# Attention of batches 2 to 7 one slot earlier in an attention + MoE kernel, with its second score half and first global scores two slots earlier

## The chip, the cores and the metric

The kernel runs on 1 core of one Trainium2 chip. The metric is device time in microseconds (us), the median of the runs shown. PE is TensorE's matmul stream, DVE VectorE, ACT ScalarE, POOL GpSimd, SP the engine whose queue issues the DMAs.

## The reference

Attention over 8 batches and 8 heads, with 512 local and 32 global positions and head dimension 64, and behind it a MoE-like layer with one expert:

```python
s_g = scale * q_g @ k_all^T;   out_g = softmax(s_g) @ v_all       # global rows see all 544 keys
s_l = concat(q_l @ k_g^T, q_l @ k_l^T where |i - j| <= 32)         # local rows: global keys and a band
out_l = softmax(s_l) @ concat(v_g, v_l)
x = concat(out_g, out_l) as (8 * 544, 512)
h = x @ w_in            # 512 -> 2048
out = (h * cos(h)) @ w_out   # 2048 -> 512
```

All is float32. The kernel keeps the accuracy by splitting operands into a high and a low float16 part, and multiplies three products (high x high, high x low, low x high) for each.

## The kernel before, in words

**MoE.** The local rows are handled in 16 chunks of 256 rows (chunk c belongs to batch c // 2), and a 17th chunk holds the global rows of all batches. A chunk has 8 blocks j, each of 256 of the 2048 hidden columns. For a block, `m1_a` (L812) makes ph with 24 matmuls of 256 columns; `m1_b` (L834, L835) and `m1_c` (the table function `Sin`, through the helper at L434) make u and w; `m1_d` squares w on POOL, multiplies into gf on DVE (L852), casts gf to gh on ACT (L856) and makes gl on POOL; `m2_a` (L872) adds 12 matmuls of 512 columns into the chunk's two output tiles po. `m2_b` evacuates po to o on DVE (L881) and ACT (L883) at the chunk's end. ph has three PSUM buffers, po two.

**Attention.** The 8 heads of a batch are four pairs p. For a pair, `sc_a` (L536) makes the scores ps, in two halves (i = 0 and i = 2), each for two heads, in fp32 on tiles of 64 rows; `sc_b` (L554) reads them on DVE with mask and running minimum; `sc_c` takes the exponentials on ACT, `sc_d` (L601, L602) the high and low planes on ACT and DVE, `sc_e` transposes them by DMA; `av_a` (L654) multiplies with the values into acc, and `av_b` (L674, L675) writes xh and xl, the input of the MoE. For two pairs g, `g_a` (L693) makes global scores gps in two parts (k = 0 of 288 and k = 1 of 256 columns), and `g_f` (L748) the global product gacc. ps, acc, gps, gacc and the small matmul pm_v (L468, `spread_b`) share the tag att, three PSUM buffers. For each batch `load_v` loads the values (one buffer vr), `v_a` takes their maximum on DVE (L490), `v_b` spreads it over the partitions by pm_v, and `v_d` makes vh on ACT and vl on DVE (L521).

**What sets the order.** Time is cut into slots. Slot 8 c + j is that of block j of chunk c, and its po matmuls stand three slots later. `at(slot, phase, f, ...)` puts each step of the attention into a slot and a phase in it. For batches 2 to 7 `steady(t)` gives a pair's slots by offsets from t, with t = 16 (b - 1) + T0 + 4 p: first score half at t - 7 (`s_sc0`), second at t - 5 (`s_sc2`), first global part at t - 6 (`s_gs0`), second at t - 4, exponentials t - 4, planes t - 3, transposes t - 1, product at t. Batch b's first MoE chunk has slot 16 b, so with T0 = 3 the last pair's product stands in the slot just before it. Batches 0 and 1 have a table of their own (`tight`). From these ranks a scheduler lays out each engine's instruction order at build time; on the chip each engine runs its own order and waits for semaphores.

```python
        for b in range(2, B):
            t = 16 * (b - 1) + T0
            for p in range(NPAIR):
                attn_pair(b, p, steady(t + 4 * p))
```

Of the kernel before, what the change touches and what calls it, by code (L numbers as in the profile page):

```python
# [8 lines left out]
F16 = mybir.dt.float16  # L9
# [5 lines left out]
AF = mybir.ActivationFunctionType  # L15
ALU = mybir.AluOpType
# [3 lines left out]
P = 128  # L20
# [4 lines left out]
D = 64  # L25
# [17 lines left out]
EXPMASK = 0x7F800000  # L43
MAGIC = 1.5 * 2.0**23
KAPPA = 3
T0 = 3
SPLIT = 256
PL = 1
MF = 1
TS = 1  # L50
# [7 lines left out]
NS = NJ // 2  # L58
# [10 lines left out]
WLV = 0  # L69
SW = 256  # L70
LO = "m01v2345"
J7 = "xl3"
L7 = -5
PS = 128
MR = 2
SR = (1,)
AR = (1,)
WH = "AAAAAAAADDDDDDDD"
# [3 lines left out]
NAL = -1.0 / math.sqrt(D)  # L82
s_load = -10
s_sc0 = -7
s_sc2 = -5
s_ex = -4
s_sd = -3
s_tr = -1
s_vd = -8
s_av = 0  # L90
s_gs0 = -6
s_gs1 = -4
s_gd = -3
s_ge = -1
# [13 lines left out]
U1 = 2  # L108
SP1 = 2
VD1 = 1  # L110
PO = 1
WOPH = 9
# [14 lines left out]

def body(tc, qf, v, wi, wo, mask, out):
    nc = tc.nc
    lag = 3  # L130

    from contextlib import ExitStack

    with ExitStack() as ctx:
# [98 lines left out]
        def decode(y, raw, s, low_after=None, join_after=None):  # L233

            hi, lo = raw.bitcast(F32)[..., 1::2], raw[..., 0::2]
            nc.scalar.activation(y, hi, AF.Prelu, scale=s, alpha=2.0**32)
            low = nc.vector.tensor_scalar(
                lo, lo, 29, 1, op0=ALU.logical_shift_right, op1=ALU.bitwise_or
            )
            behind(low.ins, low_after)  # L240
            join = nc.vector.scalar_tensor_tensor(  # L241
                y.bitcast(U32), y.bitcast(U32), 3, lo,
                op0=ALU.logical_shift_left, op1=ALU.bitwise_or,
            )
# [85 lines left out]
        def w_in_piece(k):  # L330
            kc = k // 2
            parts = wfs.pop(("raw", k))
            n = 1024 // len(parts)
            for a, raw in enumerate(parts):
                c = slice(k % 2 * 1024 + a * n, k % 2 * 1024 + a * n + n)
                z = raw.bitcast(F32)[:, 1::2]
                decode(z, raw, wfs["s", kc], join_after=J7 if k == 7 else "xs" if k == 6 else "dx" if k >= 4 else None)
                split_w(wi_h[:, kc, c], wi_l[:, kc, c], z)

        wfi = cp.tile([P, 2], F32, name="wfi")  # L340

# [64 lines left out]
        def w_out_piece(j):  # L406
            if j < 8:
                raw = wo_raw[:, j]
            else:
                raw = w2.tile([P, 1024], U32, tag="raw", name=f"raw_wo{j}")  # L410
                nc.sync.dma_start(raw.bitcast(I64), wo[j * P : (j + 1) * P])
            z = w2.tile([P, DM], F32, tag="wy", name=f"z_wo{j}")
            decode(z, raw, wsc, low_after="wsc")
            split_w(wo_h[:, j], wo_l[:, j], z, j % 4 < WLV, WH[j], SW)

        def w_out_done():
            m = ap_.tile([P, 1], F32, tag="wm", name="wm_o")
# [158 lines left out]
        def sc_d(b, p, i):  # L576
# [190 lines left out]
        mp = None  # L767
# [49 lines left out]
        def gf_tile(c, j, n):  # L817
            if GFW and c >= 2 and j % GFW == GFW - 1:
                return w2.tile([P, n], F32, tag="wy", name=f"gf_{c}_{j}")
            return mp.tile([P, n], F32, tag="gf", name=f"gf_{c}_{j}", bufs=GFB)  # L820
# [24 lines left out]
        def m1_d(c, j):  # L845
            w = st.pop(("u", c, j))[1]
            n = w.shape[-1]
            gh = mp.tile([P, n], F16, tag="gh", name=f"gh_{c}_{j}", bufs=4)
            gl = mp.tile([P, n], F16, tag="gl", name=f"gl_{c}_{j}", bufs=4)
            pool_tt(w, w, w, ALU.mult, PS if c < 2 else n)  # L850
            gf = gf_tile(c, j, n)
            nc.vector.scalar_tensor_tensor(  # L852
                gf, w, 0.5, st.pop(("ph", c, j)).rearrange("p a b -> p (a b)"),
                op0=ALU.subtract, op1=ALU.mult,
            )
            nc.scalar.copy(gh, gf)  # L856
            pool_tt(gl, gf, gh, ALU.subtract, PS if c < 2 else n)
            st["g2", c, j] = (gh, gl)

        def m2_a(c, j):  # L860
# [43 lines left out]
        def at(slot, phase, f, *a, pr=None):  # L904
            e = (phase, len(ev[slot]), f, a)
            ev[slot].append(e)
            pr = (slot, phase) if pr is None else pr if isinstance(pr, tuple) else (pr, phase)
            rank[slot, e[1]] = pr + (slot, e[1])
# [3 lines left out]
        def attn_pair(b, p, o):  # L912
            if b:
                at(o["load"], PJ, load_qk, b, p)
            attn_rest(b, p, o)

        def attn_rest(b, p, o):
            for i in range(4):
                at(o["sc"][i], PA, sc_a, b, p, i)
                at(o["sc"][i], PA if o["tight"] else PC, sc_b, b, p, i)  # L920
                at(o["ex"], PI, sc_c, b, p, i)
                at(o["sd"], PF, sc_d, b, p, i)
                at(o["tr"][i], PA2, sc_e, b, p, i)
            at(o["vd"], PF2, v_d, b, p)
            at(o["av"], PA, av_a, b, p)
            at(o["av"] if b else -6, PF, av_b, b, p)
            if p % 2:
                g = p // 2
                for k in range(2):
                    at(o["gs"][k], PA, g_a, b, g, k)  # L930
                    at(o["gs"][k], PA if o["tight"] else PC, g_b, b, g, k)
                at(o["ex"], PI, g_c, b, g)
                at(o["gd"], PF2, g_d, b, g)
                at(o["ge"], PA2, g_e, b, g)
                at(o["gf"] if b else GF0, PG, g_f, b, g)
                at(o["gf"] if b else GF0, PH2, g_g, b, g)
# [36 lines left out]
        for k in range(8):  # L973
            if 2 <= k < 4:
                at(WL[1], PJ, w_in_load, k)
            at(WE + k - WM, PH2, w_in_max, k, pr=W0 + k - WM)
            at(WE + k if k < 4 else -13 if k < 6 else -11 if k < 7 else L7, PK, w_in_piece, k, pr=(W0 + k, PJ))
            if k < 4:
                at(WE + k, PJ, w_in_load, k + 4, pr=W0 + k if k < 3 else W0 - 1)
# [5 lines left out]
            at(WOE + k // WOS if k < 12 else -10, PJ, w_out_max, k, pr=(WO + k // WOS, PI))  # L985
        at(-9, PB, w_out_done, pr=(WO + 7, PI))
        for k in range(16):
            at(k // 2 + PO, WOPH, w_out_piece, k)
        at(LV1, PJ, load_v, 1)
        at(VA1, PF, v_a, 1)  # L990
        at(VA1, PG, v_b, 1)
        at(VA1, PG2, v_c, 1)
        for p in range(NPAIR):
            attn_pair(1, p, tight(U1 + SP1 * p, VD1 + p))
        for b in range(2, B):
            t = 16 * (b - 1) + T0
            at(t + s_v, PA0, load_v, b)
# [8 lines left out]
            (-7, -4, -9, -8, -6, -2, -10),  # L1006
        )[MF]
        for c in range(NC + 1):
            at(NS * c, -11, chunk_scales, c)
            for j in range(NS):  # L1010
                s = NS * c + j
                if c == 0 and j < JS:
                    for kc in range(NPAIR):
                        at(-5 + kc, PJ, m1_a, c, j, kc)
                else:
                    at(s, ma, m1_a, c, j)
                at(s, mb, m1_b, c, j)
# [88 lines left out]
```

## Time and profile before

| | us |
|---|---|
| runs (median 951.33) | 951.33, 949.33, 951.34 |
| profiled execution, its time | 949.26 |
| span of that execution | 947.5 |
| PE busy in the span | 896.2 (95%) |
| ACT busy | 660.6 (70%) |
| DVE busy | 578.5 (61%) |
| POOL busy | 421.9 (45%) |

The span runs from the program's first instruction to the end of its last; the time of the execution holds 1.8 us beside it. Matmuls are pipelined, and a matmul's end is modelled, so that a busy PE need not be PE at its peak: in a chain of waits the start of each group, and the distance to the next one's start, tell what a group takes.

### The profile page before, as it was taken

How to read it: one execution, taken by the hardware profiler on the slowest of the kernel's cores; microseconds unless marked ns; L12 is line 12 of the kernel's file. 1: busy time of each engine (PE TensorE's matmuls, PEld its weight loads, DVE VectorE, ACT ScalarE, POOL GpSimd, SP SyncE). 2: the span in 40 equal slices, each digit the busy share in tenths (PEclk: the TensorE clock that was granted, in tenths of full speed). 3: DMA queues.
4: the chain of work that ended last, by engine and by line, in shares of the span. 5: the costliest groups of instructions: out<-in, count | busy, mean ns of one | idle time of the engine just before them, and what ended most of it. 6: DMA issues, size and time to landing. Idle time of an engine off the chain costs nothing.

```text
span 947.5 us, 19962 instructions
## 1 busy us (share of the span) xinstructions
PE 896.2 (95%) x7643; PEld 597.5 (63%) x7643; DVE 578.5 (61%) x1568; ACT 660.6 (70%) x1419; POOL 421.9 (45%) x508
## 2 busy tenths in 40 slices
PE   6757888999999999999999999999999999999995
PEld 4446564666666666666666666666666666666663
DVE  5999989757565647566656656565746555423231
ACT  6887798877787777767777677777777766434341
POOL 5867977453333243434343334324343434444441
PEclk8558999999999999999999999999999999999998
DMA  9936256645242524444352635251533333000000
GB/s 366 389 133 192 82 149 153 130 122 134 43 118 48 154 53 96 85 123 112 65 116 56 179 46 134 46 160 38 117 57 92 62 68 59 24 1 24 1 23 23
DMA packets 155176, 96.41 MB, mean 102 GB/s; under 512 B 141000, under 2 KB 141128, under 8 KB 153288
## 3 DMA queue, kind: packets, MB, share of 16 engines
q1 hardware_dynamic: 155080, 95.13, 40.2%
q8 instruction: 60, 0.98, 0.4%
q14 instruction: 36, 0.29, 0.1%
HBM read 51.59 MB, written 8.91 MB: 64 GB/s over the span
## 4 chain that ended last, share of the span: by engine, by line
PE 82%; DVE 7%; ACT 3%; POOL 3%; DMA 2%; issue 1%; SPq 0%; ACTq 0%; POOLq 0%
PE ph L812 36%; PE po L872 35%; PE ps L536 5%; PE acc L654 4%; PE gps L693 2%; DVE planes L602 1%; PE gacc L748 1%; DMA raw_wo<-wo 1%; DMA vr<-v 1%; ACT t L434 1%; POOL wo_hl L222 1%; POOL vl L518 1%; DVE z_wo L241 1%; POOL wi_l L222 1%; DVE raw_wi L241 1%
## 5 line engine op out<-in xcount | busy, mean ns | idle before, releaser
L872 PE MATMUL po<-wo_hl,gh 128*128 128x512 f16 x1088 | 321.8, 380 | 9.7 <-POOL wo_hl L222 9.7
L812 PE MATMUL ph<-xh,wi_h 128*128 128x256 f16 x1024 | 280.4, 274 | 3.3 <-DVE gf L852 3.3
L812 PE MATMUL ph<-xl,wi_h 128*128 128x256 f16 x1024 | 279.8, 273 | 0.5 <-DVE xl L675 0.5
L812 PE MATMUL ph<-xh,wi_l 128*128 128x256 f16 x1024 | 279.8, 273 | 0.0
L222 POOL TENSOR_TENSOR gl<-gf,gh 128x512 f16<-128x512 f32 (+1 forms) x184 | 173.8, 955 | 230.2 <-ACT gh L856 229.3
L222 POOL TENSOR_TENSOR w<-w 128x512 f32<-128x512 f32 (+1 forms) x184 | 152.9, 841 | 248.3 <-ACT w L434 236.0
L812 PEld LDWEIGHTS <-wi_h 128*128 128x128 f16 x2176 | 206.0, 98 | 56.2 <-issue 19.6
L872 PE MATMUL po<-wo_hl,gl 128*128 128x512 f16 x544 | 201.5, 381 | 0.0
L872 PEld LDWEIGHTS <-gh 128*128 128x128 f16 x1088 | 106.8, 98 | 103.0 <-issue 2.3
L856 ACT CAST gh<-gf 128x512 f16<-128x512 f32 x136 | 83.3, 613 | 123.8 <-DVE gf L852 122.8
L852 DVE SCALAR_TENSOR_TENSOR gf<-w,ph 128x512 f32<-128x512 f32 x136 | 93.0, 684 | 113.7 <-POOL w L222 113.0
L434 ACT ACTIVATE w<-u,ca 128x512 f32<-128x512 f32 x136 | 97.9, 721 | 87.5 <-DVE u L835 84.8
L835 DVE SCALAR_TENSOR_TENSOR u<-u,cm,ph 128x512 f32<-128x512 f32 x136 | 101.2, 744 | 94.5 <-ACT u L834 94.5
L434 ACT ACTIVATE t<-t,mn 128x192 f32<-128x192 f32 (+1 forms) x256 | 116.6, 456 | 6.4 <-DVE mn L554 6.0
L812 PEld LDWEIGHTS <-wi_l 128*128 128x128 f16 x1088 | 106.7, 98 | 14.2 <-issue 1.4
L602 DVE SCALAR_TENSOR_TENSOR planes<-t,sm,planes 128x192 f16<-128x192 f32 (+1 forms) x232 | 100.4, 493 | 13.9 <-ACT planes L601 13.2
L834 ACT ACTIVATE u<-ph,cm 128x512 f32<-128x512 f32 x136 | 92.0, 677 | 18.8 <-PE ph L812 18.8
L872 PEld LDWEIGHTS <-gl 128*128 128x128 f16 x544 | 53.3, 98 | 73.0 <-issue 10.7
L554 DVE CUSTOM_DVE_ANT_0 t<-ps,msk 128x192 f32<-128x192 f32 (+1 forms) x256 | 82.8, 366 | 11.4 <-PE ps L536 10.4
L601 ACT ACTIVATE planes<-t,sm 128x192 f16<-128x192 f32 (+1 forms) x232 | 86.1, 455 | 2.2 <-DVE gsm L720 2.2
L536 PE MATMUL ps<-qkr 64*128 64x192 f32 (+1 forms) x496 | 73.0, 382 | 6.1 <-DMA qkr<-qf 5.4
L434 ACT ACT_TABLE_LOAD x58 | 74.4, 1283 | 3.7 <-DVE u L835 2.0
(149 smaller groups left out, 919.9 us busy)
## 6 DMA issues: line engine op xcount, KB each, us to landing
qkr<-qf SPq DMA_DIRECT2D x31, 608.0 KB, 5.0
vr<-v SPq DMA_DIRECT2D x8, 1280.0 KB, 6.6
out<-o SPq DMA_DIRECT2D x34, 256.0 KB, 2.1
raw_wi<-wi SPq DMA_DIRECT2D x6, 1024.0 KB, 13.2
wo_hl<-wo SPq DMA_DIRECT2D x8, 512.0 KB, 11.5
raw_wm<-wo SPq DMA_DIRECT2D x8, 512.0 KB, 4.2
raw_wo<-wo SPq DMA_DIRECT2D x8, 512.0 KB, 4.0
raw_wi<-wi SPq DMA_DIRECT2D x4, 512.0 KB, 12.3
```

The lines of the kernel that those rows point to most:

```text
L222: nc.gpsimd.tensor_tensor(o[..., c], a[..., c], b[..., c], op=op)
L434: ins = nc.scalar.activation(*a, **k).ins
L536: nc.tensor.matmul(pt[h][:, c], q[r, QZ[j] : QZ[j] + P], k[r, z : z + w], start=True, stop=True, skip_group_check=True,)
L554: nc.vector.tensor_tensor_reduce(t[:, h], pt[h], msk[:, MOFF[i] : MOFF[i] + w], NAL, 3.0e38, ALU.add, ALU.min, mn[:, h : h + 1],)
L601: a = nc.scalar.activation(hi, t[:, h], AF.Identity, scale=r)
L602: d = nc.vector.scalar_tensor_tensor(lo, t[:, h], r, hi, op0=ALU.mult, op1=ALU.subtract)
L812: nc.tensor.matmul(ph[:, a], w[:, kc, f], x[:, kc, q], start=first and ip == 0, stop=last and ip == 2, skip_group_check=True,)
L834: nc.scalar.activation(u, ph, AF.Identity, bias=m)
L835: nc.vector.scalar_tensor_tensor(u, u, m, ph, op0=ALU.subtract, op1=ALU.subtract)
L852: nc.vector.scalar_tensor_tensor(gf, w, 0.5, st.pop(("ph", c, j)).rearrange("p a b -> p (a b)"), op0=ALU.subtract, op1=ALU.mult,)
L856: nc.scalar.copy(gh, gf)
L872: nc.tensor.matmul(po[k], g[:, a * CT + k * P : a * CT + (k + 1) * P], w[:, 2 * j + a], start=(j == 0 and i == 0), stop=(j == NS - 1 and i ...
```

## The change

Three constants: T0 from 3 to 2 moves all of the attention of batches 2 to 7 (loads of values and queries too) one slot ahead of the MoE; `s_sc2` from -5 to -6 and `s_gs0` from -6 to -7 move the second score half and the first global scores one slot more, so that a pair's two score halves stand in slots next to each other and the first global scores in the slot of the first half. The other constants (LG, LGC, GB, PSQ, PSG, SQ, GLE, WLE, WPT, WIS, U1S, VDS) have the values that stood in the code before (three slots of lag, four buffers, pieces of 128 and 256, POOL for all, the same slots).

```diff
-T0 = 3
+T0 = 2
 SPLIT = 256
+LG = 3
+LGC = 2
+GB = 4
...
-PS = 128
+PSQ = 128
+PSG = 128
+SQ = "GGGGGGGGGGGGGGGG"
+GLE = "GGGGGGGGGGGGGGGG"
+WLE = "GGGGGGGGGGGGGGGG"
+WPT = [1, 1, 2, 2, 3, 3, 4, 4, 5, 5, 6, 6, 7, 7, 8, 8]
+WIS = 256
+U1S = [2, 4, 6, 8]
+VDS = [1, 2, 3, 4]
...
 s_sc0 = -7
-s_sc2 = -5
+s_sc2 = -6
...
-s_gs0 = -6
+s_gs0 = -7
...
-            attn_pair(1, p, tight(U1 + SP1 * p, VD1 + p))
+            attn_pair(1, p, tight(U1S[p], VDS[p]))
...
+            lag = LG if c < LGC else 3
```

The order that comes of it, at three places. Names carry batch and pair or chunk and block (ps_4_1_0_0 is batch 4, pair 1, first half, head 0), and a number at the end. In the changed file the lines stand 9 to 19 later: L545 is L536, L702 L693, L821 L812, L890 L872.

PE at the start of chunk 6, the first of batch 3, before the change:

```order
L812 MATMUL ph_6_0_5461<-xh_3_4432,wi_h_86 128x256
...
L872 MATMUL po_5_1_5065<-wo_hl_88,gl_5_5_5277 128x512
L536 MATMUL ps_4_1_0_0_5502<-qkr_4_1_5273 128x192
L536 MATMUL ps_4_1_0_1_5503<-qkr_4_1_5273 128x192
L812 LDWEIGHTS wi_h_86
L812 MATMUL ph_6_0_5461<-xl_3_4433,wi_h_86 128x256
...
L536 MATMUL ps_4_1_0_0_5502<-qkr_4_1_5273 128x224
L536 MATMUL ps_4_1_0_1_5503<-qkr_4_1_5273 128x224
L812 LDWEIGHTS wi_h_86
L812 MATMUL ph_6_1_5542<-xh_3_4432,wi_h_86 128x256
```

There, and one block further on, before the change:

```order
L872 MATMUL po_5_1_5065<-wo_hl_88,gl_5_6_5346 128x512
L693 MATMUL gps_4_0_0_5583<-qkr_4_0_4952 32x288 x2
L693 MATMUL gps_4_0_0_5583<-qkr_4_1_5273 32x288 x2
L748 LDWEIGHTS vh_3_2_4436
L748 MATMUL gacc_3_1_5591<-ptg_3_1_5335,vh_3_2_4436 64x64
```

and with the change, at the start of chunk 6:

```order
L890 MATMUL po_5_1_5125<-wo_hl_88,gl_5_4_5241 128x512
L545 MATMUL ps_4_1_0_0_5445<-qkr_4_1_5237 128x192
L545 MATMUL ps_4_1_0_1_5446<-qkr_4_1_5237 128x192
L545 MATMUL ps_4_1_0_0_5445<-qkr_4_1_5237 128x224
L545 MATMUL ps_4_1_0_1_5446<-qkr_4_1_5237 128x224
L702 MATMUL gps_4_0_0_5451<-qkr_4_0_4916 32x288 x2
L702 MATMUL gps_4_0_0_5451<-qkr_4_1_5237 32x288 x2
L821 LDWEIGHTS wi_h_86
L821 MATMUL ph_6_0_5501<-xh_3_4379,wi_h_86 128x256
```

The first ph block of the chunk was begun before the po group was done, and filled in between the two windows of the scores; the global scores stood before gacc one block later. Now the whole first score half of pair 1 and the first global scores stand between po and a whole ph block.

DVE where the first score half of batch 5's pair 3 is read, before the change:

```order
L852 SCALAR_TENSOR_TENSOR gf_8_7_7506<-w_8_7_7433,ph_8_7_7407 128x512
...
L602 SCALAR_TENSOR_TENSOR planes3_82<-t_5_2_2_7392,sm_5_2_7493,planes3_82 128x192 x2
L835 SCALAR_TENSOR_TENSOR u_9_0_7535<-u_9_0_7535,cm_8_6817,ph_9_0_7510 128x512
L554 ISA t_5_3_0_7557,mn_5_3_0_7558<-ps_5_3_0_0_7551,msk_73 128x192
L554 ISA mn_5_3_0_7558 128x1
L554 ISA t_5_3_1_7561,mn_5_3_1_7562<-ps_5_3_0_0_7551,msk_73 128x224
L554 ISA mn_5_3_1_7562 128x1
L554 ISA t_5_3_0_7557,mn_5_3_0_7558<-ps_5_3_0_1_7552,msk_73 128x192
...
L500 TENSOR_REDUCE vs_6_7589<-pm_v6_7587 128x1
...
L852 SCALAR_TENSOR_TENSOR gf_9_0_7598<-w_9_0_7536,ph_9_0_7510 128x512
```

and with the change:

```order
L867 SCALAR_TENSOR_TENSOR gf_8_6_7457<-w_8_6_7384,ph_8_6_7358 128x512
...
L611 SCALAR_TENSOR_TENSOR planes3_82<-t_5_2_2_7285,sm_5_2_7444,planes3_82 128x192 x2
L844 SCALAR_TENSOR_TENSOR u_8_7_7486<-u_8_7_7486,cm_8_6857,ph_8_7_7461 128x512
L563 ISA t_5_3_0_7513,mn_5_3_0_7514<-ps_5_3_0_0_7502,msk_73 128x192
L563 ISA mn_5_3_0_7514 128x1
L563 ISA t_5_3_1_7517,mn_5_3_1_7518<-ps_5_3_0_0_7502,msk_73 128x224
L563 ISA mn_5_3_1_7518 128x1
L563 ISA t_5_3_0_7513,mn_5_3_0_7514<-ps_5_3_0_1_7503,msk_73 128x192
...
L715 ISA gt_5_1_7521,gmn_5_1_7522<-gps_5_1_0_7508,zero_74 128x288
...
L867 SCALAR_TENSOR_TENSOR gf_8_7_7557<-w_8_7_7487,ph_8_7_7461 128x512
L509 TENSOR_REDUCE vs_6_7548<-pm_v6_7546 128x1
```

The reads and vs_6 (the maximum that pm_v spreads) stand one MoE block earlier, at block 7 of chunk 8 and no longer at block 0 of chunk 9, and the global scores are read right behind them. On PE pm_v6 stood behind these scores, and now stands behind the 17th matmul of ph_9_0.

DVE where batch 6's values are taken up, before the change:

```order
L521 SCALAR_TENSOR_TENSOR vl_5_3_7490<-vr_5_6077,vs_5_6218,vh_5_3_7489 128x640
L764 SCALAR_TENSOR_TENSOR xg_97<-gacc_4_1_6962,pvs_98,xg_97 128x2x32
L835 SCALAR_TENSOR_TENSOR u_8_2_7040<-u_8_2_7040,cm_8_6817,ph_8_2_7015 128x512
L881 TENSOR_SCALAR o_7_1_7058<-po_7_1_6436,co_6_5447 128x512
L797 TENSOR_SCALAR co_10_8189<-osc_96,pvs_98 128x1
...
L490 TENSOR_REDUCE vm_6_7583<-vr_6_7448 128x1
L852 SCALAR_TENSOR_TENSOR gf_8_2_7084<-w_8_2_7041,ph_8_2_7015 128x512
```

and with the change:

```order
L530 SCALAR_TENSOR_TENSOR vl_5_3_7441<-vr_5_6028,vs_5_6177,vh_5_3_7440 128x640
L773 SCALAR_TENSOR_TENSOR xg_97<-gacc_4_1_6926,pvs_98,xg_97 128x2x32
L844 SCALAR_TENSOR_TENSOR u_8_1_7004<-u_8_1_7004,cm_8_6857,ph_8_1_6979 128x512
L499 TENSOR_REDUCE vm_6_7542<-vr_6_7399 128x1
L867 SCALAR_TENSOR_TENSOR gf_8_1_7029<-w_8_1_7005,ph_8_1_6979 128x512
```

The maximum vm_6 came after u_8_2, the evacuation of po_7_1 and two score reads; now it comes after u_8_1 alone, and gf_8_1 behind it.

## Rows read from the trace of the kernel before

**Rows 1.** The page of the profile, its head and part 1: span, then PE's busy time, share of the span and count of instructions.

```profile
span 947.5 us, 19962 instructions
...
PE 896.2 (95%) x7643; PEld 597.5 (63%) x7643; DVE 578.5 (61%) x1568; ACT 660.6 (70%) x1419; POOL 421.9 (45%) x508
```

**Rows 2.** Busy time by stretches of 20 us, of the whole program: start:end, length, then busy us of PE, PEld, DVE, ACT and POOL with their instruction counts, the granted TensorE clock, the DMA share and GB/s.

```profile
140.00:160.00 20.00, 15.75 (x129) 9.97 (x125) 18.53 (x44) 17.54 (x40) 15.72 (x28) 0.91 0.73 182
160.00:180.00 20.00, 19.67 (x160) 11.59 (x160) 16.05 (x50) 19.45 (x47) 11.09 (x25) 1.00 0.50 131
180.00:200.00 20.00, 20.00 (x192) 13.62 (x191) 11.54 (x31) 15.57 (x33) 8.90 (x20) 1.00 0.45 70
...
500.00:520.00 20.00, 20.00 (x203) 12.91 (x200) 12.95 (x35) 14.10 (x30) 7.76 (x7) 1.00 0.28 54
...
860.00:880.00 20.00, 20.00 (x140) 13.48 (x138) 6.50 (x9) 8.22 (x13) 8.32 (x8) 1.00 0.07 27
```

**Rows 3.** The list of waits, PE's rows: who waited <- for whom, us in total, times, longest us.

```profile
PE po L872 <- POOL wo_hl L222: 9.7, 6, 2.6
...
PE ph L812 <- DVE gf L852: 3.3, 3, 2.2
```

**Rows 4.** The chain of waits from 404 to 441 us, the first blocks of chunk 6, in order of time: start us, us, engine, tile, line and count.

```profile
404.43 0.65 PE po L872 x3
405.07 0.53 PE ps L536 x4
405.60 0.65 PE ph L812 x5
406.25 0.58 PE ps L536 x4
406.83 2.73 PE ph L812 x24
409.56 2.59 PE po L872 x12
412.15 0.62 PE gps L693 x8
412.77 0.74 PE gacc L748 x40
413.51 2.73 PE ph L812 x24
...
418.82 0.90 PE ps L536 x8
...
425.04 1.29 PE acc L654 x36
426.34 0.57 PE gps L693 x8
...
438.44 2.62 PE ph L812 x24
```

**Rows 5.** The chain of waits from 551 to 559 us: the product of batch 5's pair 1 (acc) and the first score half of pair 3 (ps).

```profile
551.35 1.29 PE acc L654 x36
...
557.96 0.90 PE ps L536 x8
```

**Rows 6.** DVE's timeline at 562.5 us, in order of time: start us, us, engine, line, operation, tiles, shapes. These are its two reads of the first head of the scores that end in rows 5.

```profile
562.51 0.34 DVE L554 CUSTOM_DVE_ANT_0 t<-ps,msk 128x192 f32<-128x192 f32 x1
...
562.79 0.38 DVE L554 CUSTOM_DVE_ANT_0 t<-ps,msk 128x224 f32<-128x224 f32 x1
```

**Rows 7.** ACT's timeline from 553.6 to 560.4 us (the bracket is idle time before, and what ended it): the last exponential of pair 2's scores, u, xh, a table load, w and the eight planes.

```profile
553.59 0.44 ACT L434 ACTIVATE t<-t,mn 128x192 f32<-128x192 f32 x1
...
554.02 0.67 ACT L834 ACTIVATE u<-ph,cm 128x512 f32<-128x512 f32 x1
554.59 0.67 ACT L674 ACTIVATE xh<-acc,xs 128x512 f16<-128x512 f32 x1
555.55 1.28 ACT L434 ACT_TABLE_LOAD   x1 [0.28 <-DVE u L835]
556.85 0.72 ACT L434 ACTIVATE w<-u,ca 128x512 f32<-128x512 f32 x1
557.47 2.97 ACT L601 ACTIVATE planes<-t,sm 128x192 f16<-128x192 f32 x8
```

**Rows 8.** DVE's timeline from 518 to 528 us: vl of batch 5's last pair, u of the next block, and the maximum over batch 6's values, which the load into the same buffer releases.

```profile
518.19 0.88 DVE L521 SCALAR_TENSOR_TENSOR vl<-vr,vs,vh 128x640 f16<-128x640 f32 x1
...
519.55 0.75 DVE L835 SCALAR_TENSOR_TENSOR u<-u,cm,ph 128x512 f32<-128x512 f32 x1 [0.28 <-ACT u L834]
...
525.35 2.82 DVE L490 TENSOR_REDUCE vm<-vr 128x1 f32<-128x2560 f32 x1 [3.35 <-DMA vr<-v]
```

**Rows 9.** The view of the tile vr, its last row: from the issue of a load of values to its landing.

```profile
DMA to landing us min/median/max: 5.3/6.6/11.1
```

**Rows 10.** The page of the profile, part 5: the squares on POOL; busy us, mean ns of one | idle before.

```profile
L222 POOL TENSOR_TENSOR w<-w 128x512 f32<-128x512 f32 (+1 forms) x184 | 152.9, 841 | 248.3 <-ACT w L434 236.0
```

**Rows 11.** DVE's timeline at 177.8 us: four planes of batch 1's pair 3 in one row.

```profile
177.80 2.01 DVE L602 SCALAR_TENSOR_TENSOR planes<-t,sm,planes 128x192 f16<-128x192 f32 x4 [2.03 <-ACT planes L601]
```

**Rows 12.** The chain of waits at 172.5 us: two groups of second-layer matmuls of chunk 1.

```profile
172.51 5.18 PE po L872 x24
```

More of the change, by code (lines that the diff above doesn't have):

```diff
@@ L129, in body @@
     nc = tc.nc
-    lag = 3
     from contextlib import ExitStack
@@ L337, in w_in_piece @@
                 decode(z, raw, wfs["s", kc], join_after=J7 if k == 7 else "xs" if k == 6 else "dx" if k >= 4 else None)
-                split_w(wi_h[:, kc, c], wi_l[:, kc, c], z)
+                split_w(wi_h[:, kc, c], wi_l[:, kc, c], z, n=WIS)
         wfi = cp.tile([P, 2], F32, name="wfi")
@@ L413, in w_out_piece @@
             decode(z, raw, wsc, low_after="wsc")
-            split_w(wo_h[:, j], wo_l[:, j], z, j % 4 < WLV, WH[j], SW)
+            split_w(wo_h[:, j], wo_l[:, j], z, WLE[j] == "D", WH[j], SW)
         def w_out_done():
@@ L847, in m1_d @@
             n = w.shape[-1]
-            gh = mp.tile([P, n], F16, tag="gh", name=f"gh_{c}_{j}", bufs=4)
-            gl = mp.tile([P, n], F16, tag="gl", name=f"gl_{c}_{j}", bufs=4)
-            pool_tt(w, w, w, ALU.mult, PS if c < 2 else n)
+            gh = mp.tile([P, n], F16, tag="gh", name=f"gh_{c}_{j}", bufs=GB)
+            gl = mp.tile([P, n], F16, tag="gl", name=f"gl_{c}_{j}", bufs=GB)
+            e = SQ[NS * c + j] if c < 2 else "G"
+            if e == "A":
+                nc.scalar.activation(w, w, AF.Square)
+            elif e == "D":
+                nc.vector.tensor_tensor(w, w, w, op=ALU.mult)
+            else:
+                pool_tt(w, w, w, ALU.mult, PSQ if c < 2 else n)
             gf = gf_tile(c, j, n)
@@ L856, in m1_d @@
             nc.scalar.copy(gh, gf)
-            pool_tt(gl, gf, gh, ALU.subtract, PS if c < 2 else n)
+            if c < 2 and GLE[NS * c + j] == "D":
+                nc.vector.tensor_tensor(gl, gf, gh, op=ALU.subtract)
+            else:
+                pool_tt(gl, gf, gh, ALU.subtract, PSG if c < 2 else n)
             st["g2", c, j] = (gh, gl)
@@ L987, in body @@
         for k in range(16):
-            at(k // 2 + PO, WOPH, w_out_piece, k)
+            at(WPT[k], WOPH, w_out_piece, k)
         at(LV1, PJ, load_v, 1)
```

## The prediction

> **What bounds the kernel now.** I read the page first, then the busy time by stretches, then the chain of waits, and last the timelines of ACT and DVE at the places where the change could make TensorE wait.
>
> The page gives PE 896.2 of 947.5 us [rows 1]. A busy share alone could hide waits, because the ends of matmuls are modelled, so I looked at where the idle part lies. By stretches PE is short of full only in the first 165 us: 15.75 of 20 between 140 and 160, 19.67 between 160 and 180, and full from 180 us on, as in the middle (500 to 520) and in the pure MoE part at the end (860 to 880) [rows 2]. The waits of PE that matter are a few us, for pieces of the output weights and for gf [rows 3]; both lie in the first part, since later slices have no idle time.
>
> The chain of waits then shows what PE's time is made of once it is saturated [rows 4]. A block of 24 first-layer matmuls (ph) takes 2.62 us if second-layer matmuls (po) stand before it, and 12 po take 2.59. Behind any attention work the same ph block takes 2.73. So **each time PE goes from MoE work to attention work and back costs 0.11 us** beyond the attention work itself. And a run of score matmuls (ps) has a fixed cost: eight in one run take 0.90, but cut in two they take 0.53 and 0.58, which is 0.21 more. At 404 to 407 us stands such a cut: po x3, ps x4, ph x5, ps x4, ph x24. It comes from the first block of a new batch: its last pair's activations are not ready when PE gets there, so the order fills in other work.
>
> So from about 165 us on the end moves only with two things: what PE executes (fixed, but for these seams), and any wait that the new order puts before PE.
>
> **The change part by part.** All other constants of the diff repeat the old values; three act: T0 (all attention of batches 2 to 7 a slot earlier), s_sc2 (second score half one slot earlier still) and s_gs0 (first global scores likewise). No instruction is added or removed, SP's order of DMAs and transposes is the same row by row, and ACT has 58 table loads in both orders.
>
> *Seams on PE.* I counted both orders from the first matmul of ph_1_5 (chunk 1, j = 5; PE is saturated from there) to the end. Stretches of attention work between MoE work: 95 before, 79 now. The first global scores now stand right behind the pair's first score half instead of a stretch of their own, and the cuts at the batch starts are gone, since the last pair's product now comes a block earlier. 16 x 0.11 = 1.76 us less. Runs of ps: 56 before, 50 now: 6 x 0.21 = 1.26 us less. **Together -3.0 us.**
> The seam ps to gps (global scores) does not occur in the saturated part of the trace. Bounds from the nearest rows: a seam between two kinds of attention work costs nothing more where it shows (acc 1.29 and gps 0.57 back to back; gps 0.62 and gacc 0.74 back to back [rows 4]); at worst each of the 12 costs the 0.11 of a seam, which would leave -1.7. Nothing suggests a gain there. I take zero, as in the nearest rows.
> The Trainium skill (TensorEngine Tiling (Array Packing), Tiling Modes, Key Properties) says that the array is drained whenever the tiling mode changes. By that rule seams between two kinds of attention work cost too, and what counts is changes of mode: from the orders 215 before, 193 now. That result is the second rival.
>
> *The scale matmul in the middle of ph.* The order now puts pm_v of the next batch 17 ph matmuls behind the first global scores of pair 3. It takes the PSUM buffer of the first head's scores, so PE waits there until DVE has read them. PE wants it 0.62 + 17 x 2.62/24 = 2.5 us after the scores end. Before, scores ended at 557.96 + 0.90 = 558.86 [rows 5] and DVE finished the first head's two reads at 563.17 [rows 6], 4.3 us later, because DVE came late from the planes, which wait for ACT. So with an unchanged lag: 1.8 us in each of 5 batches, 9 us. The other end is zero. I take zero, since the lag gets shorter: before, xh could start only at 554.59, though acc had ended at 551.35 + 1.29 = 552.64, because ACT was still at the pair's exponentials until 554.03 and then at u [rows 5, 7]. The scores' second half now comes a slot sooner, and in ACT's new order all eight exponentials, gh and u stand ahead of where acc ends. That is 1.95 us, and the table load behind it no longer waits its 0.28 us for DVE [rows 7]. 4.3 - 1.95 - 0.28 = 2.1 against 2.5 us: 0.4 us to spare.
>
> *DVE's maximum over the next values (vm, 2.82 us) goes ahead of gf.* Before, vl ended at 519.07 and vm began at 525.35 [rows 8]: the load into the same buffer takes 6.3 us, and DVE used part of it for other work. Now only xg and u stand between, so DVE idles longer, and behind it wait gf_8_1, u_8_2, o_7_1 (the evacuation that the next chunk's po needs). From the end of gacc, DVE comes to the end of o after some 1.2 (xg, vl) + 6.3 + 2.8 + 2.7 (u 0.75 [rows 8], gf and o as long, 0.5 for small ones) = 13.0 us. PE needs it after 2.73 + 2.59 + 2.62 + 2.59 + 1.29 + 0.57 + 2.73 + half a po group 1.3 = 16.4 us. **Hidden, with 3.4 us to spare**; without that cover it would be 5 batches times what is over. It lies on the landing time, 6.6 us median and 11.1 at most [rows 9].
>
> *ACT: w of j = 2 now behind the planes.* From acc's end: xh 0.7, planes 3.0, global exponentials 0.7, table 1.3, w 0.7 [rows 7] (the global one taken as long as w), its square on POOL 0.84 [rows 10], u and gf on DVE 1.4: about 8.7 us. The ph block that needs this buffer starts 0.57 + 2.73 + 2.59 + 0.90 + 2.73 + 2.59 + 0.90 = 13.0 us after acc. Hidden.
>
> *The ramp.* Before 165 us the order changes by single places: vl of batch 2 (0.88 us) goes ahead of a weight cast on DVE. DVE is full there, so it is worth between -0.9 and +0.9 [rows 8]; I take zero. Just behind it, DVE now reads the second head of batch 2's first scores after three of four planes, by 177.80 + 3/4 x 2.01 + 0.7 = 180.0 [rows 6, 11], and gacc_1_0 waits for that read; PE comes to it at about 172.51 + 5.18 + 2 x 0.90 + 0.55 = 180.0 [rows 12]. The next product waits for DVE likewise. Between 0 and 1.0 us, once; I take 0.4.
>
> **Sum:** -1.76 - 1.26 + 0.4 = -2.6 us. The profiled execution took 949.26 (span 947.5), so 946.6 in its terms. The three runs shown are 951.33, 949.33 and 951.34: the profile lies 2.07 below their median, at the lower of two levels. Against the median: 951.33 - 2.6 = **948.7**. A measurement of this kernel tells 0.2% (1.9 us) from no change.
>
> **The rivals.**
> 1. *Small waits eat the gain* (0.18). DVE reads for pm_v 0.7 us later than I reckon, so that PE waits 0.3 in each of 5 batches, and the ramp costs its 1.0: -3.0 + 1.5 + 1.0 = -0.5, 950.8. For it: 0.4 us to spare is thin. Against: DVE is busy 12.95 and ACT 14.10 of 20 us there [rows 2], so neither is late for long.
> 2. *Every change of mode costs* (0.05). The cut in rows 4 has two changes more than the whole run and costs 0.21 + 0.65 - 5 x 2.62/24 = 0.31, so 0.16 a change; 22 fewer make -3.5, with the ramp -3.1: 948.2. Against it: in the row's sums acc before gps costs no more than its own 1.29 [rows 4]. By the Trainium skill's rule on tiling modes, named above, it would be so; the trace does not bear that out (1.29).
> 3. *The seams are no time at all, or come back at ps to gps and in the ramp* (0.09): within 1 us of 951.3.
> 4. *Slower by the scale matmul* (0.08). If ACT's exponentials end more than about 1 us later than I put them, xh starts no earlier than before, the lag stays 4.3 us, and PE stands 1.8 us in each of 5 batches: -2.6 + 9.2 = +6.6, 957.9. It decides when the lag exceeds 2.5 us. For it: ACT is the engine that DVE waits for there. Against: the scores are there a slot earlier.
> 5. *Slower by the value load* (0.05). With landings near the 11.1 us maximum, o is 4.5 us later, 1.1 over the cover, 5 times: -2.6 + 5.5 = +2.9, 954.2.
>
> **How the numbers follow.** The forecast has 0.55. Faster by over 0.2%: forecast and rival 2, 0.60. Same: rivals 1 and 3, 0.27. Slower: rivals 4 and 5, 0.13. The range starts at the lower level of the runs with the whole gain and the better end of the ramp, 949.33 - 3.0 - 0.9 = 945.4, and goes up to the level of 951.34 with 0.7 us for the worse ends of the same cases, 952.0; it leaves out rivals 4 and 5 and a little of the others. On its own the forecast has 946.2 to 949.5.
>
> **What would show it.** Right: in the chain of the changed kernel the period from one batch to the next falls by some 0.5 us (two seams and a cut), ph blocks at chunk starts are whole, gps stands behind ps x8 with nothing between, and PE is still full in every stretch from 180 us on. Wrong: PE idle before pm_v with DVE as its releaser (rivals 1, 4); PE's po waiting for o with DVE's vm late behind its load (rival 5); ps to gps with 0.1 us more than 0.90 and 0.62 (rival 3); a gap before gacc_1_0 or acc_1_2 near 180 us over 1 us.

## The result, and the profile after

The change is slower: **955.90 us median** (954.13 to 961.0, 7 runs) against 950.42 of before beside it; ratio 1.0069, 95% interval [1.0056, 1.0083]. The forecast was 948.7. The profiled execution took 957.83 (span 956.1).

The head of the page of the changed kernel, and its waits (PE's rows: who waited <- for whom, us, times, longest), against [rows 1, 3]:

```profile
span 956.1 us, 19961 instructions
...
PE 894.2 (94%) x7643; PEld 597.6 (63%) x7643; DVE 578.1 (60%) x1568; ACT 659.0 (69%) x1419; POOL 421.6 (44%) x508
```

```profile
PE po L890 <- POOL wo_hl L231: 9.9, 5, 4.5
...
PE pm_v L477 <- DVE mn L563: 8.0, 5, 2.3
```

PE is busy 2.0 us less than before and the span is 8.6 longer. One row is new: five waits at pm_v for DVE's read of the scores, 8.0 us. Among the rows of before, the only one for the scores' read is this, at the scores themselves, both times in the first 17 us:

```profile
PE ps L536 <- DVE mn L554: 0.6, 2, 0.4
```

PE around the fourth of them, in batch 5 (timeline: start us, us, engine, line, operation, tiles, shapes, count; the bracket is idle time before it):

```profile
559.59 0.97 PE L545 MATMUL ps<-qkr 64*128 64x192 f32 x8
560.49 0.69 PE L702 MATMUL gps<-qkr 128*32 128x288 f32 x8
561.12 0.28 PE L821 MATMUL ph<-xh,wi_h 128*128 128x256 f16 x1
...
564.65 0.22 PE L477 MATMUL pm_v<-d_v,ones 128*128 128x128 bf16 x1 [1.50 <-DVE mn L563]
```

The scores end where gps starts, at 560.49. The forecast let PE come to pm_v 2.5 us later, at 563.0, and DVE be done by then. DVE's two reads of the first head say otherwise (DVE's timeline, same columns):

```profile
563.27 0.73 DVE L844 SCALAR_TENSOR_TENSOR u<-u,cm,ph 128x512 f32<-128x512 f32 x1
563.93 0.34 DVE L563 CUSTOM_DVE_ANT_0 t<-ps,msk 128x192 f32<-128x192 f32 x1
...
564.21 0.38 DVE L563 CUSTOM_DVE_ANT_0 t<-ps,msk 128x224 f32<-128x224 f32 x1
```

They end at 564.59, a **lag of 4.1 us** behind the scores. Before had 4.3 in that batch by [rows 5, 6] (4.4 if the scores' end is read from PE's timeline, as it is here and from here on), and the forecast had 2.1.

What made DVE late is in the chain of waits that ends at this pm_v (start us, us, what; rows between are left out). It goes back over 40 us:

```profile
522.41 5.73 DMA vr<-v
...
528.16 2.82 DVE vm L499
530.98 0.61 DVE gf L867
...
531.61 0.63 ACT gh L871
...
549.26 0.72 ACT w L443
...
550.00 1.28 ACT L443
...
551.29 1.40 ACT t L443 x6
...
555.52 0.59 ACT u L843
...
558.89 2.63 ACT planes L610 x7
...
561.53 1.82 DVE planes L611 x5
563.35 0.66 DVE u L844
564.01 0.27 DVE t L563
...
564.65 0.22 PE pm_v L477
```

DVE stands at vm until the next batch's values have landed; gf_8_1 is queued behind vm, and gh, which ACT casts from it, behind gf. From there every step comes late, block after block, to the exponentials (551.29), the planes and the reads. Between 533.47 and 538.50 the chain names no releaser; ACT's timeline shows ACT at work all that time, from gh through xh, the planes, a global exponential and a table load to w. PE notices nothing until pm_v.

A second loss follows the longest wait, 2.3 us in batch 3. There the chain has `358.33 4.28 PE po L890 x12` for a group that takes 2.59, and the windows of 1 us show why (start:end, length, busy us of PE, PEld, DVE, ACT, POOL with counts, granted TensorE clock, DMA share, GB/s):

```profile
356.00:357.00 1.00, 0.00 (x0) 0.00 (x0) 1.00 (x5) 0.19 (x1) 1.00 (x1) 1.00 1.44 140
...
358.00:359.00 1.00, 1.00 (x7) 0.50 (x5) 0.59 (x3) 0.00 (x0) 0.65 (x1) 0.74 1.07 222
359.00:360.00 1.00, 1.00 (x4) 0.31 (x3) 0.93 (x5) 0.60 (x2) 0.00 (x0) 0.50 1.09 210
```

After PE had stood, the granted clock was 0.50, the 1.2 GHz level, for some 3 us: 1.7 us more.

The seams came as forecast. The chain of waits from 605 to 616 us, where scores and gps stand together:

```profile
605.22 1.29 PE acc L663 x36
606.51 2.73 PE ph L821 x24
609.24 2.59 PE po L890 x12
611.83 0.90 PE ps L545 x8
612.73 0.62 PE gps L702 x8
613.36 2.73 PE ph L821 x24
```

ps 0.90 and gps 0.62 are the times that each has alone [rows 4]: the seam between them costs nothing.

To weigh all of it I took PE's groups from start to start. The 156th po matmul, near 196 us, divides the ramp from the rest: ahead of it stands the same number of matmuls of every kind in both orders. From there on each group of the change is compared with the same group of experiment 9 below, which has the change's order on PE and no wait of PE there; what experiment 9 takes less than before is put down to the seams:

| profiled executions, after less before | forecast, us | measured, us |
|---|---|---|
| ramp, to the 156th po matmul | +0.4 | +0.8 |
| excess of the ph groups with pm_v | 0 | +8.8 |
| lowered clock behind one of them | none | +1.7 |
| small excesses | none | +0.2 |
| seams (experiment 9 less before) | -3.0 | -3.0 |
| sum | -2.6 | +8.5 (957.83 - 949.26 = 8.57) |

### The profile page after: what moved, and what is told of

It is laid out like the page before. It is cut to its first block, busy times and chain, and to the rows that moved or that the text cites. A ratio compares the mean times of both kernels' runs of the same rounds, so it can differ in the third digit from the quotient of the medians.

```text
span 956.1 us, 19961 instructions
## 1 busy us (share of the span) xinstructions
PE 894.2 (94%) x7643; PEld 597.6 (63%) x7643; DVE 578.1 (60%) x1568; ACT 659.0 (69%) x1419; POOL 421.6 (44%) x508
## 4 chain that ended last, share of the span: by engine, by line
PE 49%; ACT 10%; DVE 8%; issue 7%; POOL 6%; DMA 2%; ACTq 0%; POOLq 0%; DVEq 0%
PE po L890 22%; PE ph L821 21%; ACT t L443 3%; POOL w L231 3%; ACT planes L610 2%; PE ps L545 2%; POOL gl L231 2%; DMA vr<-v 2%; PE acc L663 2%; DVE gf L867 2%; ACT L443 2%; DVE u L844 2%; ACT gh L871 1%; DVE planes L611 1%; DVE vl L530 1%
## 5 line engine op out<-in xcount | busy, mean ns | idle before, releaser
L890 PE MATMUL po<-wo_hl,gh 128*128 128x512 f16 x1088 | 323.6, 382 | 9.9 <-POOL wo_hl L231 9.9
L821 PE MATMUL ph<-xh,wi_h 128*128 128x256 f16 x1024 | 280.6, 274 | 2.3 <-DVE gf L867 2.3
L821 PE MATMUL ph<-xl,wi_h 128*128 128x256 f16 x1024 | 279.8, 273 | 0.5 <-DVE xl L684 0.5
L821 PE MATMUL ph<-xh,wi_l 128*128 128x256 f16 x1024 | 279.8, 273 | 0.0
L821 PEld LDWEIGHTS <-wi_h 128*128 128x128 f16 x2176 | 207.0, 98 | 58.2 <-issue 19.0
L890 PE MATMUL po<-wo_hl,gl 128*128 128x512 f16 x544 | 202.8, 382 | 0.0
L890 PEld LDWEIGHTS <-gh 128*128 128x128 f16 x1088 | 107.1, 98 | 104.7 <-issue 4.4
L844 DVE SCALAR_TENSOR_TENSOR u<-u,cm,ph 128x512 f32<-128x512 f32 x136 | 101.0, 743 | 98.1 <-ACT u L843 98.1
L821 PEld LDWEIGHTS <-wi_l 128*128 128x128 f16 x1088 | 106.7, 98 | 22.4 <-issue 9.6
L611 DVE SCALAR_TENSOR_TENSOR planes<-t,sm,planes 128x192 f16<-128x192 f32 (+1 forms) x232 | 94.9, 472 | 22.4 <-ACT planes L610 22.4
L890 PEld LDWEIGHTS <-gl 128*128 128x128 f16 x544 | 53.5, 98 | 73.8 <-issue 12.2
L545 PE MATMUL ps<-qkr 64*128 64x192 f32 (+1 forms) x496 | 71.1, 378 | 6.0 <-DMA qkr<-qf 5.7
```

Source lines behind the costliest of these rows:

```text
L545: nc.tensor.matmul(pt[h][:, c], q[r, QZ[j] : QZ[j] + P], k[r, z : z + w], start=True, stop=True, skip_group_check=True,)
L611: d = nc.vector.scalar_tensor_tensor(lo, t[:, h], r, hi, op0=ALU.mult, op1=ALU.subtract)
L821: nc.tensor.matmul(ph[:, a], w[:, kc, f], x[:, kc, q], start=first and ip == 0, stop=last and ip == 2, skip_group_check=True,)
L844: nc.vector.scalar_tensor_tensor(u, u, m, ph, op0=ALU.subtract, op1=ALU.subtract)
L890: nc.tensor.matmul(po[k], g[:, a * CT + k * P : a * CT + (k + 1) * P], w[:, 2 * j + a], start=(j == 0 and i == 0), stop=(j == NS - 1 and i ...
```

## The experiments

Two questions: is the loss those waits, and what makes DVE late? Ratios are against before beside each run; an excess is what PE's groups take beyond their usual time from 196 us on, and the rest is what remains there against before. I call **lag** the time from the scores' end (pair 3, first half) to the end of DVE's second read of their first head, as read from the timelines.

**1. pm_v one slot later** (e1_pmv_later)

```diff
-            at(t + s_v + 1, PG, v_b, b)
-            at(t + s_v + 1, PG2, v_c, b)
+            at(t + s_v + 2, PG, v_b, b)
+            at(t + s_v + 2, PG2, v_c, b)
```

> The change, with pm_v and vs of batches 2 to 7 one slot later: pm_v stands no longer in the middle of a ph block but behind gacc, a slot after the pair's first scores. Theory A (the loss is TensorE's wait at pm_v, 8.0 us in the profile of the changed kernel, and what the lowered clock behind one of them costs, 1.6; the seams gave their 3.0): no wait before pm_v over 0.5 us, no stretch of lowered clock after 180 us, and the median 955.9 goes to 946.5 to 948.5. Rival B (pm_v only shows a lateness that TensorE meets at the next step anyway, or the loss lies in the ramp and the value load): 953 to 956. Rival C (the waits cost what A says but the seams gave nothing): 950 to 951.

Measured: 958.79, ratio 1.0102 [1.0084, 1.0120]. No theory foresaw that. The wait did not go; it moved behind gacc, where pm_v takes the buffer of the next scores:

```profile
PE pm_v L477 <- DVE mn L563: 8.3, 5, 1.9
```

The excesses sum to 12.6 (with 1.5 of lowered clock once), the rest to -2.9. The edit tested another place of the same wait, not its absence.

**2. Global scores where they were** (e2_no_gs0)

```diff
-s_gs0 = -7
+s_gs0 = -6
```

> The change without its third constant: the first global scores stay one slot behind the first score half (s_gs0 = -6), so that pm_v takes the third PSUM buffer right behind the scores and waits for no read. 89 attention stretches instead of 79, 50 score runs as in the change. Theory A (the wait at pm_v is the loss, and it comes from gps taking the third buffer): no wait before pm_v, 950.4 - 6 x 0.11 - 6 x 0.21 = 948.5, up to 950.4 if the ramp's 1.9 is real. Rival B (lateness met at the next step, the score half of i = 2, which needs both first buffers): a wait at ps instead, 953 to 956.

Measured: 955.30, 1.0062 [1.0046, 1.0078]. pm_v waits no more, but the same late reads (lag 4.6 to 4.9) show at gacc, which takes the next buffer:

```profile
PE gacc L757 <- DVE mn L563: 2.0, 5, 0.9
```

PE's excesses come to 5.8 (2.0 of it in four runs of the second score half, nearly all else in the ph groups ahead of gacc), the rest is -1.9 as counted, and the ramp of this execution took 2.5 more than that of before. Rival B was right that the lateness is met at the next step, and named a third of it.

**3. Exponentials a slot sooner** (e3_ex_sooner)

```diff
-s_ex = -4
+s_ex = -5
...
-                at(o["ex"], PI, g_c, b, g)
+                at(o["ex"] + (not o["tight"]), PI, g_c, b, g)
```

> The change, with the exponentials of a pair's local scores one slot earlier (s_ex = -5, the global ones stay), so that they end before the product of the pair ahead; pm_v stays in the middle of ph. The theory for the step that failed: the lag from the scores to DVE's reads is set by ACT, whose exponentials end 0.65 us after acc and whose table load of 1.28 follows xh; both go ahead of acc here. Then the lag of 4.1 us falls by 1.7 (xh right behind acc) to 3.0 us (the table load gone from there too), to between 1.1 and 2.4, below the 2.5 that TensorE has to spare: waits at pm_v under 1 us in all, 947 to 949.5. There are 24 table loads more on ACT, which has idle time. Rival (DVE's planes or POOL set the lag, not ACT's exponentials): lag 3.5 to 4.1, waits of 1 to 1.7 us in each of 5 batches, 953 to 956.

Measured: 975.03, 1.0267 [1.0249, 1.0285]; lag 3.6 to 4.6. My theory of that hour fell: with the exponentials out of the way, xh still came 3.5 us after acc, which ended at 563.03 there (ACT's timeline):

```profile
565.45 0.62 ACT L871 CAST gh<-gf 128x512 f16<-128x512 f32 x1 [1.87 <-DVE gf L867]
565.97 0.68 ACT L843 ACTIVATE u<-ph,cm 128x512 f32<-128x512 f32 x1
566.55 0.68 ACT L683 ACTIVATE xh<-acc,xs 128x512 f16<-128x512 f32 x1
```

xh stands in ACT's queue behind gh, and gh waits for gf: the MoE's own chain was late. The edit also brought 24 table loads (82 against 58) and new waits.

**4. The other two constants alone** (e4_sc_gs_only): `T0 = 3` in the change.

> The change without its first constant: T0 = 3 as before, only the second score half and the first global scores sooner. pm_v stands 17 matmuls inside a ph block here too; 83 attention stretches instead of 95, 56 score runs. Theory A: the lag is that of before, 4.3 to 4.4 us, or 0.3 longer than in the change; TensorE waits 1.8 to 1.9 us at pm_v in each of 5 batches, 9 to 9.5 in all, and the seams give 12 x 0.11 = 1.3: 958 to 960 with what the clock loses behind the waits. Rival B (the loss is of the slot that all attention moves, the ramp and the value load): within 1.5 us of before, 949 to 952.

Measured: 957.84, 1.0091 [1.0070, 1.0113]; lag 4.3 to 4.6, waits 9.0 us in all, the rest -1.3. The mechanism is theory A's, seams included, and the time lies just under its range; the slot that T0 moves is not needed for the loss.

**5. pm_v one slot sooner** (e5_pmv_sooner): `t + s_v` in place of `t + s_v + 1` for v_a, v_b and v_c, so that vm comes a slot sooner too.

> The change, with the maximum over the next values, pm_v and vs in the slot of the value load, one slot sooner: pm_v stands behind the product acc of pair 1, ahead of pair 3's scores, and takes a PSUM buffer that nothing is late for. The first try to take the wait away (pm_v one slot later) only moved it: there pm_v took the buffer of the second score half's first head, and TensorE stood 1.5 to 2.0 us behind gacc instead. Theory A (the whole difference is the seams' -3.1 and the waits at pm_v with what the clock loses behind them): no wait at pm_v, no excess over 0.3 us per group after 185 us, and before's median less 2 to 3.5 us, 946 to 948 where before has 949.4 to 950.4. Rival B (the late DVE reads hold up the next step, the second score half, which needs the same buffer): waits of 0.5 to 1 us at ps, 949 to 953. Rival D (the ramp of this order is 1.5 to 3 us longer, whatever comes later): 948.5 to 951.

Measured: 955.11, 1.0055 [1.0041, 1.0068]. None of the three ranges holds it. pm_v waits for no read, yet the time is hardly better: DVE's vm still stood 5.3 us for its load, and PE now waited for the evacuations o.

```profile
PE po L890 <- ACT o L901: 4.7, 5, 1.3
...
PE po L890 <- DVE o L899: 2.0, 4, 0.9
```

Excesses 9.1, the rest -3.0. So the wait at pm_v is where the lateness shows and not its source: each of the variants so far met late work somewhere.

**6. No loads of values** (e6_no_vload; the values of batch 1 are used in every later batch, which changes what is computed)

```diff
         def load_v(b):
+            if b > 1:
+                st["vr", b] = st["vr", 1]
+                return
```

> The change, without the loads of values for batches 2 to 7 (the values of batch 1 are used again, which changes the output); all else of the values' work stays. It takes away what DVE's maximum vm waits for, 4.9 us with gf_8_1 queued behind it. The question is what keeps DVE's reads of the scores late. Theory V (the chain that ends at pm_v goes back to vm's wait through gf, gh and ACT's work behind them, and never catches up): the lag from the scores' end to the first head's read falls from 4.1 us by 1.4 us or more (ACT's idle time before gh_8_1), waits at pm_v under 0.5 us each, 947 to 950. Rival W (ACT's own load from the exponentials on sets it: table load, eight exponentials, xh, table load, w, eight planes): the lag stays within 0.5 us of 4.1, the waits at 1 to 2.4 us each, 953 to 957.

Measured: 960.68, 1.0113 [1.0100, 1.0126], in neither range; the lag is theory V's, 2.2 to 2.8, and the row of pm_v is

```profile
PE pm_v L480 <- DVE mn L566: 0.2, 1, 0.2
```

The time is lost in the ramp: the 181st po matmul, near 213 us before, comes 14.3 us later, and from there to the end this kernel takes 3.4 less than before. The work on the values crowds in early there (seven maxima on DVE by 135 us, three in the change); that this is what costs the time was not tested. The total alone would have misled.

**7. T0 alone** (e7_t0_only): `s_sc2 = -5`, `s_gs0 = -6` in the change.

> The first constant alone: T0 = 2, the second score half and the first global scores stand as far from the rest of the attention as before. 88 attention stretches instead of 95 and 50 score runs instead of 56; pm_v right behind the scores, on a free buffer. Theory A: -7 x 0.11 - 6 x 0.21 = -2.0 us and no wait, so 947.4 to 949 against before's 949.4 to 950.4. Rival D (the ramp of T0 = 2 is 1.5 to 3 us longer): 949 to 951. Rival B (all attention a slot sooner is itself late for TensorE): 953 to 956.

Measured: 955.27, 1.0061 [1.0044, 1.0078]. pm_v is free here, and the wait is at gps behind acc, for score reads that stand behind vm in DVE's queue. The number lies in rival B's range; experiment 12 tests rival B's reading of it. PE's waits, then DVE's timeline:

```profile
PE gps L702 <- DVE mn L563: 6.4, 3, 2.7
```

```profile
522.79 2.82 DVE L499 TENSOR_REDUCE vm<-vr 128x1 f32<-128x2560 f32 x1 [5.80 <-DMA vr<-v]
525.52 0.38 DVE L563 CUSTOM_DVE_ANT_0 t<-ps,msk 128x224 f32<-128x224 f32 x1
```

**8. The change once more** (e8_change_again)

> The change itself once more, beside the others on the same chip, with a second profile. Theory A: waits at pm_v of 1 to 2.4 us in 5 batches again, 7 to 9 us, 954 to 957; the lowered clock behind a wait, 1.7 us once in the first profile, may or may not be there, and so may the 1.5 us of the ramp. Rival (the first profile's waits were of that execution): under 4 us of waits in this profile.

Measured: 956.68, 1.0069 [1.0056, 1.0081]; waits at pm_v 7.7 us, ramp +1.5, no group with the lowered clock.

**9. vm at another place in DVE's queue** (e9_vm_behind_gf): the change, with one ordering edge, and `st["gfi", c, j]` kept for gf.

```diff
-                nc.vector.tensor_reduce(
+                r = nc.vector.tensor_reduce(
...
+                if b > 2:
+                    tc.add_manual_dep(r.ins, st["gfi", 2 * (b - 2), VJ].ins.name, order, reason="max_behind_gf")
```

with VJ = 5.

> The change with one instruction of DVE per batch (from batch 3 on) at another place: the maximum vm over the next values no longer ahead of gf of block 1 of a batch's first chunk, where DVE stood 4.9 us until the values had landed, but behind gf of block 5, where DVE had 3.2 us without work. PE's order stays. Theory V (without the loads, the lag from the scores to DVE's read fell from 3.6-4.9 to 2.2-2.8 us, so that the wait at pm_v comes from vm's wait for its load, passed on through gf, gh and ACT's work for 35 us): lag 2.2 to 2.8, waits at pm_v of 0 to 0.4 us each from batch 4 on, the seams' -3.1 stay: 946.5 to 948.5 where before has 949.5, and so faster than before and the change. Rival W (without the loads it was the emptier queues and ports, not vm's place): lag 3.6 or more, 953 to 956. Rival X (vm's 2.8 us push what stands behind it there, the sums and u, as far back): lag 3 to 4, 950 to 953.

Measured: **947.08**, 0.9964 [0.9952, 0.9976]: faster than before and than the change. vm runs in DVE's gap with no wait, xh follows acc, and no wait of PE over 0.15 us is left after 185 us. The chain around pm_v, ACT at acc's end and DVE in batch 5:

```profile
545.10 1.29 PE acc L666 x36
...
551.71 0.90 PE ps L548 x8
552.61 0.62 PE gps L705 x8
553.24 1.96 PE ph L824 x17
555.20 0.06 PE pm_v L478
```

```profile
544.86 0.44 ACT L444 ACTIVATE t<-t,mn 128x192 f32<-128x192 f32 x1
...
546.43 0.69 ACT L686 ACTIVATE xh<-acc,xs 128x512 f16<-128x512 f32 x1
```

```profile
542.11 2.81 DVE L500 TENSOR_REDUCE vm<-vr 128x1 f32<-128x2560 f32 x1
...
554.59 0.38 DVE L566 CUSTOM_DVE_ANT_0 t<-ps,msk 128x224 f32<-128x224 f32 x1
```

The exponentials end at 545.30, before acc does at 546.39; xh starts at 546.43. This is the picture that the forecast had drawn for the change.

**10. vm behind gf of block 3** (e10_vm_behind_gf3): VJ = 3.

> As the run before it in this list, with vm behind gf of block 3, a place where DVE has no gap: u of block 4 and the reads of a second score half are due there. The values have landed by then, so vm waits for nothing and only takes its 2.8 us. If the load's wait is what counts (theory V), the lag stays below 3.3 us and the time within 1.5 us of the run before. If DVE's time at the wrong place counts as much as the wait, the lag is 3.5 us or more and the waits at pm_v return, 950.5 to 955.

Measured: 954.53, 1.0038 [1.0024, 1.0051]; lag 3.1 to 4.0, and

```profile
PE pm_v L478 <- DVE mn L566: 5.4, 5, 1.4
```

With the values landed vm waits for nothing here, and its 2.8 us at a place without a gap still cost 6.2 us of excess at pm_v, against 8.8 in the change. So it is not the DMA as such: what counts is whether DVE's queue is held ahead of a gf or u.

**11. The same in the kernel before** (e11_before_vm_later): an edge of the same kind, behind the read of the second score half.

> The kernel before, with vm moved in the same manner (behind the last read of the second score half of the batch's pair 2, where DVE has 3.2 us without work). In it no wait of TensorE over 0.15 us is left after 185 us, though DVE's reads lag there too (2.2 to 4.9 us), because TensorE does not come back to their buffer for 6 us. Theory V with the seams: no gain, 949 to 950.5 as before. Rival (DVE's wait costs in any order, and the change's gain is not the seams): 947 or less here too.

Measured: 950.38, 1.0000 [0.9990, 1.0009], though its lag fell to 2.2 in every batch. In the kernel before the lateness was there and cost nothing.

**12. T0 alone, with vm moved** (e12_t0_vm_later): experiments 7 and 11 together.

> The first constant alone (T0 = 2, as in the run t0_only, 955.27 against 949.7) with vm moved behind the last read of the second score half of the batch's pair 2, where DVE has 3.2 us without work. There pm_v stood on a free buffer, and TensorE waited 1.5 to 2.7 us three times at gps behind acc for score reads that stood behind vm in DVE's queue. Theory V (any order that needs DVE within some 3 us of a batch's start pays for vm's wait, wherever the wait shows): no wait over 0.3 us after 185 us, the seams' -2.0 (7 x 0.11 + 6 x 0.21) come through, less up to 1 us of ramp: 947.5 to 949.5 against before's 950.4. Rival (moving all attention a slot sooner is late for TensorE by itself): 952 to 956.

Measured: 947.87, 0.9981 [0.9968, 0.9994]; no wait over 0.15 us after 185 us, the rest -2.0, ramp +0.5. The waits at gps went with vm's wait.

| lag by batch 2 to 6, us | | time against before, us |
|---|---|---|
| before | 2.2, 3.6, 4.0, 4.4, 4.9 | |
| the change | 4.0, 4.9, 4.5, 4.1, 3.6 | +5.5 |
| 9: vm in DVE's gap | 2.2, 2.4, 2.3, 2.4, 2.3 | -3.3 |
| 10: vm without a gap | 3.1, 4.0, 3.7, 4.0, 3.7 | +4.2 |
| 11: before, vm in the gap | 2.2, 2.2, 2.2, 2.2, 2.2 | 0.0 |

## Why the prediction was wrong

**Seams: right.** -3.0 forecast; experiment 9, where no excess clouds it, takes 3.0 less than before from 196 us on (17 stretches and six runs of ps fewer there, 3.1 at the forecast's prices), its period from batch to batch falls from 101.5 to 101.0, experiment 12 takes 2.0 less where 2.0 was counted, and experiment 4's rest is -1.3 where 1.3 was. ps to gps costs nothing, as taken. The second rival, a price for every change of mode, finds no support in the rows at 605 to 613 us.

**The scale matmul: this step failed.** The forecast took the lag from 4.3 to 2.1, "since the lag gets shorter". Its place, price and point of decision stood in the fourth rival (0.08): beyond 2.5 us PE stands, 9.2 us at an unchanged lag, 957.9; measured 8.8 in one profile and 8.6 in the other, 955.9. The order was read rightly: the exponentials, gh and u do stand ahead of xh. But an order tells no time. The first group behind acc on PE, then ACT's last exponential, xh and the table load:

```profile
554.27 0.28 PE L821 MATMUL ph<-xh,wi_h 128*128 128x256 f16 x1
```

```profile
554.48 0.44 ACT L443 ACTIVATE t<-t,mn 128x192 f32<-128x192 f32 x1
...
556.01 0.67 ACT L683 ACTIVATE xh<-acc,xs 128x512 f16<-128x512 f32 x1
556.97 1.28 ACT L443 ACT_TABLE_LOAD   x1 [0.28 <-DVE u L844]
```

ACT came to the exponentials only at 551.29, behind w and a table load, and they ended 0.65 us after acc instead of before it; then gh and u, and xh came 1.74 after acc (2.0 before the change, read in the same way). The "1.95 us" so shrank to 0.3. The forecast's second term, the table load's 0.28 us of waiting for DVE's u, did not go either: the row has it unchanged. The forecast also took what bound ACT from the row nearest to the event [rows 7] and did not go further back.

**vm ahead of gf: hidden only where I looked.** The 3.4 us to spare were reckoned to one reader, the evacuation o; o held nobody up for long in the change. The other way out of the same queue, gf to gh to ACT, was not followed; experiments 6 and 9 show that vm's place brought some 2 us of lateness to pm_v, 35 us later, and the chain above shows the way it took. So the two terms that the prediction priced apart, vm's place and the lag at pm_v, were one.

**w behind the planes: hidden**, as said; no wait for it shows.

**The ramp:** +0.8 and +1.5 in the profiles of the change, against the 0.4 taken and an end of 1.9. Profiles of orders with T0 = 3 range from -0.2 to 0.9 there, those with T0 = 2 (without experiment 6) from -0.2 to 2.8. About 1 us may be the change's; single executions do not settle it.

**The lowered clock** was in no term. Between 185 and 935 us it came in these runs only behind a wait of PE.

**What stays open:** the lag in the kernel before grows from 2.2 to 4.9 over the batches. DVE's wait at vm grows there too, from 2.2 to 3.8 us (3.35 for batch 6's values [rows 8]), and with vm moved the lag stays at 2.2 (experiment 11), so the growth comes by way of vm; why the wait at vm grows was not looked into.

## What to carry to other kernels

A new place for a matmul asks two questions: when does PE come, and how late is the engine that frees its buffer; answer the second by following that engine's own chain back to its start, even 40 us, and not from the last row before it. DVE, waiting for a DMA, held its whole queue here, and lateness that costs nothing in one order is the first thing that a tighter order pays for: look for it in idle rows of engines that "do not matter". When a wait that has been removed comes back elsewhere at the same size, stop moving its victim and look for its source; here one instruction in a gap of DVE turned +5.5 us into -3.3.

## What the runs showed of the hardware

- A wait of PE can lower its clock for longer than the wait. Behind 2.3 us of standing the granted clock was 0.50 for some 3 us and a po group took 4.28 in place of 2.59; in experiment 1 a wait of 1.9 cost 1.5 more, and in experiment 7 one of 2.7 was followed by 0.50 and a ph group of 4.39 in place of 2.73. It is not certain: in experiment 8 a wait of 2.3 in the same place was followed by a clock of 1.00 (its window from 358 us):

```profile
358.00:359.00 1.00, 1.00 (x10) 0.69 (x9) 0.66 (x4) 0.00 (x0) 1.00 (x1) 1.00 1.25 267
```

  The Trainium skill (TensorE: Matmul & The Clock Gate, Part 1: The HAM clock gate) says that the moment at which the clock rises under sustained work shifts from run to run. These two traces do not show that; they show a clock that falls in one execution (0.50) and does not in the other (1.00), and no run here shows why.
- Two kinds of matmul on different tiles of the array, fp32 scores of 64 rows and global scores of 32 columns, follow each other at no cost (0.90 and 0.62), while leaving MoE work and coming back costs 0.11 each time (a ph block of 2.73 in place of 2.62 [rows 4]); the -3.0 of experiment 9 bears out the sum of them.
